# A Fourier-mixing block and its MLP: the first phase's loads, modulation rows, sequence matrices and negated halves in another order

## The chip, the cores and the metric

The kernel runs on one core of a Trainium2 chip. The metric is the time of one execution in microseconds (us) as the device counts it, median of several runs. Engines are called as the profile does: PE is TensorE (PEld its weight loads), DVE is VectorE, ACT is ScalarE, POOL is GpSimd, SP is SyncE, which only issues DMAs.

## The reference

Sequence length 2048, width 1024, MLP width 3584, all float32. The inputs are x, two pairs of DFT matrices (sequence and hidden), the MLP's weights and biases, a condition vector `c` and `w_mod`.

```
mod = (silu(c) @ w_mod).reshape(6, ...)
sa, ca, ga, sb, cb, gb = mod
h = layernorm(x) * (1 + ca) + sa
a = einsum("sd,ed->se", h, dft_hid_re);  b = einsum("sd,ed->se", h, dft_hid_im)
x = x + ga * (dft_seq_re @ a - dft_seq_im @ b)
h = layernorm(x) * (1 + cb) + sb
x = x + gb * (gelu(h @ w1 + b1) @ w2 + b2)
```

## The kernel before

All of it stands in one function, `fast()`. Work is written as small tasks, each with an engine, an assumed cost, the keys it waits for and a due time; a planner picks among the streams of tasks the one to emit next, and so fixes the order of each engine's queue at build time. Each engine works through its queue in that order. On-chip memory is one arena addressed by hand: `XR`, `EO`, `CRING`, `WRING`, `COP` and so on are offsets in it, and a task that writes a place waits for the last reader of what lay there before. SyncE issues nearly all loads; a load that must wait for its place holds up all loads behind it.

The first phase is what the change touches. It runs in these steps.

1. **Loads and mod.** Sixteen tiles of x (`load_x`, L2485, 128 x 1024 each), of which eight have a place at a time, and eight loads `wm` (L2496, 128 x 2048 each: the columns of `w_mod` for sa and ca). `mod_part` multiplies them by silu(c), part on TensorE, part on VectorE (L2534), which gives the shift and scale of the first LayerNorm as columns (L2584 to L2588).
2. **LayerNorm and folds.** The tiles are normalised, transposed by TensorE (L2685) and shifted and scaled. They are folded by their symmetry: `folds(cls)` adds and subtracts halves on VectorE (L2753, L2759, L2772) for two classes of sequence positions, ScalarE makes the fp16 high half of the result (L2778) and VectorE the low half (L2780). Key `("hop", cls, loc)` says that a part of the hidden operand is there.
3. **Modulation rows.** `row(n, j)` builds one row of mod (n = 0 to 3: ga, cb, sb, gb), spread over all partitions. Each row takes eight loads of 128 x 1024 (L2881, m = 0 to 31 in all) and eight pairs of float32 matmuls (L2887) that add up in one pair of PSUM banks. Key `("wru", m)` says that the place of load m has been read, `("rowe", n)` that row n was copied out. The loads go round in the places `WRING`. The gb row (n = 3) stands in the sequence stage and uses banks 0 and 1.
4. **Hidden DFT.** Eighteen units (`hid_unit`, L2956), each some 18 or 30 matmuls of fp16 in three passes (high times high, high times low, low times high); ScalarE and VectorE split each result again into fp16 halves (L2519, L2522). That is the right operand of the sequence DFT.
5. **Sequence matrices.** `cop_item` loads parts of the cosine and sine matrices in eight items (L2830) through the places `CRING`, two small ones (`dsp`, `csp`, L2795, L2811) before them, and splits them into fp16 halves at `COP`. The ring has six places, so that the last items wait until earlier ones were split (`("cru", n)`).
6. **Sequence DFT.** Sixteen tiles (`seq_tile`): 12 or 13 matmuls Q (L3038) and 24 to 26 matmuls P (L3026); ScalarE copies Q (L3043), VectorE forms P - Q and P + Q (L3048, L3053). The tiles 4 to 7 and 12 to 15 need part of the sequence matrix with the other sign. `neg_tasks` negates those parts in place on ScalarE (L2999), four instructions after tile 3 and four after tile 11, so tiles 4 and 12 wait for them.
7. **Second LayerNorm.** Pairs of finished tiles are multiplied by ga, added to x, normalised (L3097, L3115 to L3148), transposed (L3158), split (L3188, L3197, L3210). Each token's x + gb * b2 is stored too, where gb is needed (`gbb`).

Then the MLP: first layer (L3590) and second layer (L3699) as products of combined blocks in fp16 halves, with the splits of weights and activations on ScalarE (L2372) and VectorE (L2384, L2397), and the scales of the second layer (L3680). Both run on TensorE to the end of the kernel.

## Time and profile before

| what | value |
|---|---|
| median of 3 runs | 1428.72 us (1420.83 to 1430.15) |
| profiled execution, its own time | 1430.01 us |
| its span in the trace | 1428.2 us |
| mean granted clock of TensorE | 0.955 |
| busy: TensorE, VectorE, ScalarE, GpSimd | 1295.8, 1092.2, 749.7, 259.7 us |
| DMA moved | 302.30 MB, 212 GB/s over the span |
| first class-0 fold on VectorE (L2753) | at 72.87 us |
| first hidden matmul (L2956) | at 119.81 us |
| first sequence matmul (L3038) | at 188.94 us |
| first matmul of the MLP (L3590) | at 343.66 us |
| first second-layer scale delivered (L3680), eviction (L3739) | 428.59 us |

The page divides the span into 40 slices of 35.7 us and gives the busy share of each engine in tenths. A row of the timeline reads: start, duration, engine, line, operation, what it writes and reads, how many instructions were merged, and in brackets how long the engine stood idle before and what ended that. A row of windows gives, for a stretch of the span, its length, the busy time and number of instructions of each engine, TensorE's granted clock, the busy share of the DMA engines and the rate.

### The profile page before, as it was taken

What the parts mean: (1) busy time and instruction counts of PE and PEld (TensorE: products, weight loads), DVE (VectorE), ACT (ScalarE), POOL (GpSimd) and SP (SyncE); (2) the same over time, 40 slices, a digit from 0 to 9 for tenths busy, and PEclk for the clock granted to TensorE, in tenths of its full rate; (3) what the DMA queues carried; (4) which work ended last, traced back from release to release, by engine and by line L of the source; (5) the groups of instructions that cost most, each with busy time, mean ns of one, the idle gap of its engine ahead of it and who ended that gap; (6) DMA issues with size and microseconds to landing.
All of it is one profiled execution on the core that took longest, in us unless ns stands there. A gap on an engine that the chain in (4) does not pass through costs nothing.

```text
span 1428.2 us, 17336 instructions
## 1 busy us (share of the span) xinstructions
PE 1295.8 (91%) x6081; PEld 620.9 (43%) x6081; DVE 1092.2 (76%) x1623; ACT 749.7 (52%) x1188; POOL 259.7 (18%) x421
## 2 busy tenths in 40 slices
PE   5788588876969999999999999989999999999987
PEld 2545255543424444444444444434444444444433
DVE  5977677969697789889899897546585858675885
ACT  4685347776866746455555433346535353626330
POOL 2000010002101101010000000344534333543301
PEclk9899598998999999999999999999999999999999
DMA  9872334568456955676353546998877787876725
GB/s 369 322 251 83 88 134 91 157 216 310 142 204 192 255 164 183 204 186 216 137 181 125 192 172 240 305 314 282 287 261 249 241 279 261 281 254 209 235 81 112
DMA packets 108107, 302.30 MB, mean 212 GB/s; under 512 B 13900, under 2 KB 13900, under 8 KB 106088
## 3 DMA queue, kind: packets, MB, share of 16 engines
q1 hardware_dynamic: 75656, 195.63, 39.2%
q0 software_dynamic: 32352, 105.45, 24.9%
q8 instruction: 49, 0.80, 0.2%
q14 instruction: 50, 0.41, 0.1%
HBM read 216.10 MB, written 84.93 MB: 211 GB/s over the span
## 4 chain that ended last, share of the span: by engine, by line
PE 58%; DVE 4%; DMA 3%; issue 2%; ACT 1%; POOL 0%; SPq 0%; DVEq 0%; POOLq 0%; ACTq 0%
PE ps L3699 31%; PE ps L3590 26%; DVE arena L2384 1%; DMA arena<-in_cre_dram 1%; DVE arena L3749 1%; DMA arena<-in_w_dram 1%; DMA arena<-fw 1%; DVE arena L2397 1%; ACT arena L2372 1%; DMA fw<-arena 1%; DVE arena L3616 0%; POOL out_dram L3801 0%; POOL arena L3521 0%; ACT arena L3609 0%; ACT ps L3288 0%
## 5 line engine op out<-in xcount | busy, mean ns | idle before, releaser
L3590 PE MATMUL ps<-arena 128*128 128x512 f16 x2352 | 522.0, 384 | 28.8 <-ACT arena L3612 16.8
L3699 PE MATMUL ps<-arena 128*128 128x512 f16 x2352 | 515.4, 381 | 18.1 <-ACT arena L3739 14.2
L3590 PEld LDWEIGHTS <-arena 128*128 128x128 f16 x2352 | 232.7, 99 | 314.3 <-issue 42.9
L3699 PEld LDWEIGHTS <-arena 128*128 128x128 f16 x2352 | 231.1, 98 | 300.1 <-issue 25.1
L3749 DVE SCALAR_TENSOR_TENSOR arena<-ps,i4c,arena 128x1024 f32<-128x1024 f32 x179 | 229.4, 1282 | 101.6 <-PE ps L3699 98.5
L2372 ACT ACTIVATE arena<-arena,shc 128x512 f16<-128x512 f32 (+1 forms) x115 | 116.3, 1018 | 161.6 <-DVE arena L2397 94.2
L2384 DVE SCALAR_TENSOR_TENSOR arena<-arena,shc 128x512 f16<-128x512 f32 (+1 forms) x115 | 129.0, 1122 | 35.3 <-ACT arena L2372 34.9
L2397 DVE TENSOR_TENSOR arena<-arena 128x512 f32<-128x512 f32 (+1 forms) x196 | 149.1, 764 | 3.5
L3495 ACT ACTIVATE arena<-arena 128x512 f32<-128x512 f32 (+5 forms) x148 | 91.2, 617 | 104.9 <-DVE arena L3504 93.7
L3609 ACT ACTIVATE arena<-arena,b1s,i1c 128x512 f32<-128x512 f32 x78 | 63.4, 813 | 91.2 <-DVE arena L3616 91.2
L3504 DVE TENSOR_TENSOR arena<-arena 128x256 f32<-128x256 f32 x240 | 88.5, 420 | 14.8 <-DMA arena<-in_cre_dram 14.8
L3300 POOL PARTITION_ALL_REDUCE sums<-sums x21 | 11.0, 523 | 487.5 <-DVE sums L3296 487.5
L3616 DVE TENSOR_TENSOR arena<-arena,ps 128x512 f32<-128x512 f32 x78 | 53.4, 685 | 53.1 <-PE ps L3590 49.9
L2372 ACT ACTIVATE arena<-arena,s1c 128x512 f16<-128x512 f32 (+1 forms) x70 | 61.0, 885 | 59.8 <-DVE arena L2397 44.2
L2887 PE MATMUL ps<-arena,scol 128*128 128x512 f32 x128 | 63.6, 649 | 14.1 <-DMA arena<-in_wm_dram 11.2
L2384 DVE SCALAR_TENSOR_TENSOR arena<-arena,s1c 128x512 f16<-128x512 f32 (+1 forms) x70 | 66.5, 960 | 12.6 <-ACT arena L2372 12.4
L3521 POOL DMA_DIRECT2D arena<-in_cim_dram x99 | 53.7, 542 | 102.9 <-ACT arena L3495 97.1
L2384 DVE SCALAR_TENSOR_TENSOR arena<-arena,s2c 128x1024 f16<-128x1024 f32 x49 | 62.1, 1281 | 9.1 <-ACT arena L2372 9.0
L3521 POOL DMA_DIRECT2D arena<-in_cre_dram x99 | 54.2, 548 | 78.1 <-ACT arena L3495 58.8
L3288 ACT ACTIVATE ps<-arena 128x1024 f32<-128x1024 f32 x46 | 46.9, 1019 | 32.7 <-DMA arena<-in_w_dram 24.7
L3612 ACT ACTIVATE arena<-ps 128x512 f32<-128x512 f32 x78 | 45.9, 589 | 31.8 <-PE ps L3590 31.7
L2956 PE MATMUL ps<-arena 128*128 128x257 f16 (+5 forms) x297 | 45.8, 303 | 17.7 <-DVE arena L2522 10.5
(204 smaller groups left out, 1226.4 us busy)
## 6 DMA issues: line engine op xcount, KB each, us to landing
fw<-arena SPq DMA_DIRECT2D x73, 512.0 KB, 5.7
arena<-fw SPq DMA_DIRECT2D x112, 256.0 KB, 5.4
arena<-fw SPq DMA_DIRECT2D x49, 512.0 KB, 5.5
arena<-in_cre_dram POOLq DMA_DIRECT2D x96, 256.0 KB, 5.1
arena<-in_cim_dram POOLq DMA_DIRECT2D x96, 256.0 KB, 5.1
arena<-in_wm_dram SPq DMA_DIRECT2D x32, 512.0 KB, 5.8
arena<-in_w_dram SPq DMA_DIRECT2D x56, 256.0 KB, 4.4
arena<-in_w_dram SPq DMA_DIRECT2D x28, 512.0 KB, 6.3
```

The lines of the kernel that those rows point to most:

```text
L2372: act.activation(o[m][0], q(j), AF.Copy, **sc)
L2384: dve.scalar_tensor_tensor(o[m][1], q(j), scale, o[m][0], op0=ALU.mult, op1=ALU.subtract)
L2397: dve.tensor_tensor(q(d), q(a), q(b), op=op)
L2887: pe.matmul(bank((6 if n < 3 else 0) + h), scol[:, k : k + 1].to_broadcast([P, P]), FA(o + 512 * h, (1, 512)), start=k == 0, stop=k == 7,)
L3495: f = lambda: act.activation(sq(a), sq(a), AF.Square, accum_out=csum[0:pn, n : n + 1])
L3504: dve.tensor_tensor(a[:, o::2], a[:, o::2], b[:, o::2], op=op)
L3521: return lambda t: gp.dma_start(t[0:pn], v)
L3590: pe.matmul(ps.rearrange("p (k t) -> p k t", k=4), w1c[:, m, s, a, d * P : (d + 1) * P], zc(m)[:, b, :, d, :], start=(start and d == 0 and ...
L3609: act.activation(dst, src, AF.Gelu_apprx_tanh, scale=inv, bias=b1s[:, 2 * p + j : 2 * p + j + 1])
L3616: after_pe("dve", 0.6, lambda: dve.tensor_tensor(q, q, ps[b], op=ALU.add), kp[b])
L3699: pe.matmul(t[:, j], hidc[:, c_, m, a, k * P : (k + 1) * P], w2c[:, m, c_, w], start=(start and c_ == 0 and n == 0), stop=(c_ == 1 and n = ...
L3749: lambda: dve.scalar_tensor_tensor(dst, ps[b], inv, dst, op0=ALU.mult, op1=ALU.add), kp[b],
```

## The change

Line numbers shift: what stood at L2485 stays there, the wm loads move to L2499, row loads to L2885, row matmuls to L2891, sequence matrix loads to L2829, folds to L2752 to L2779, hidden matmuls to L2958, negations to L3004, sequence matmuls to L3032 and L3044, first and second layer to L3596 and L3705.

- x tiles 4 to 7 and 8 to 11 are loaded after the second and the fifth wm load, not behind all of them.
- `CRING` gets two more places (31984 and 33008, where x tiles lay); only the last two items, which take the places of the two small ones, wait for an earlier item to be split.
- Rows 2 and 3 load into other places: loads 16 to 19 into the second ring, 20 to 23 into freed places of normalised tiles and of x, 24 to 31 into the class-0 part of `EO` after the class-0 folds. The gb row's matmuls move to the hidden stage, into banks 6 and 7.
- The split of a class-0 fold waits for row load 11 and no longer for 19; that of class 1 waits for the last x tiles and two sequence items.
- The hidden units of a class come in another order: by `loc` first.
- The negated halves are written to places of their own (`NEG`), the first four before the first sequence tile, the other four after tile 7; tiles 4 to 7 and 12 to 15 read from there.
- Due times, the assumed cost of a row's matmuls (0.88 to 0.46), the place of gb's copy and of b2, and the waits of some later loads go with it.

```diff
-    CRING = (41996, 49172, 0, 1028, 2056, 3084)
+    CRING = (41996, 49172, 0, 1028, 2056, 3084, 31984, 33008)
-    WRING = [25792 + 1024 * n for n in range(4)], [34656 + 1024 * n for n in range(4)], (4160, 5184, 6208)
-    GBT = 19072
+    WRING = [25792 + 1024 * n for n in range(4)], [34656 + 1024 * n for n in range(4)]
+    GBT, B2T = 29920, 30944
-    COP = (102400, 69632)
+    COP, NEG = (102400, 69632), (8320, 102400)
...
     for k in range(8):
+        if k == 2 or k == 5:
+            for i in range(4 if k == 2 else 8, 8 if k == 2 else 12):
+                load_x(i)
         load(("wm", k), lambda k=k: sp.dma_start(wm2(k), wm[:, k, 0 : 2 * D]), cost=2.75)
-    for i in range(4, 8):
-        load_x(i)
...
-        o = CRING[n if n < 2 else (n - 2) % 6]
+        o = CRING[n if n < 2 else n % 8]
-        free = {0: [], 1: [], 2: [("cru", 0), *w1_made], 3: [("cru", 1)]}
-        deps = free.get(n, [("n", 11)] if n < 8 else [("cru", n - 6)])
+        free = {0: [], 1: [], 8: [("cru", 0), *w1_made], 9: [("cru", 1)]}
+        deps = free.get(n, [("n", 11)] if n < 6 else [("n", 15)])
...
-            h = add(f"foldh{cls}", "act", 2.0, ..., [ka, ("wru", 23 if cls else 19)], None, due)
+            h = add(f"foldh{cls}", "act", 2.0, ..., [ka, *(([("n", 15), ("wru", 23)] + [("cru", 6), ("cru", 7)] * loc) if cls else [("wru", 11)])], None, due)
...
-            split("cop", src, hi, lo, SC, [key, ("wru", 15), ("tpd", 3)], last, 1024, 58.0 + ch)
+            split(f"cop{ch // 2}", src, hi, lo, SC, [key, ("wru", 19), ("wru", 21), ("tpd", 3)], last, 1024, 38.0 if ch == 2 else 58.0 + ch)
...
-            elif 20 <= m < 24:
-                o, was = xr(m - 16), [("n", 15)]
+            elif m < 16:
+                o, was = WRING[m // 4 % 2][m % 4], [("wru", m - 8)] if m > 7 else w1_made
+            elif m < 20:
+                o, was = WRING[1][k], [("wru", m - 4)]
+            elif m < 22:
+                o, was = nr(m - 11), [("tpd", 2)]
             elif m < 24:
-                o, was = WRING[m // 4 % 2][m % 4], [("wru", m - 8)] if m > 7 else w1_made
+                o, was = xr(m - 18), [("n", 13)]
             else:
-                o, was = WRING[2][m % 3], [("wru", m - 3)] if m > 26 else hidend
+                o, was = eo(k // 4, k % 4, 0, 0), [("hop", 0, 0), ("hop", 0, 1)]
-                        bank((6 if n < 3 else 0) + h), scol[:, k : k + 1].to_broadcast([P, P]), FA(o + 512 * h, (1, 512)),
+                        bank(6 + h), scol[:, k : k + 1].to_broadcast([P, P]), FA(o + 512 * h, (1, 512)),
-            if k == 0 and n == 3:
-                deps.append(("y", 10))
-            add("rowp", "pe", 2 * FP, f, deps, ("wru", m), (45.0, 45.0, 39.0, 205.0)[n])
+            add("rowp", "pe", 2 * FR, f, deps, ("wru", m), (39.0, 39.0, 39.5, 63.0)[n])
...
-        for tp in range(2):
-            for t in range(2):
+        for loc in range(2):
+            for tp in range(2):
                 for c_ in range(2):
-                    hid_unit(tp, t, cls, c_)
+                    hid_unit(tp, tp ^ loc, cls, c_)
...
-                    "neg", "act", 1.0, lambda v=v: act.activation(v, v, AF.Copy, scale=-1.0),
-                    [("P", 8 * tp + 3), ("Q", 8 * tp + 3)], ("neg", tp, t, a), 75.0 + 11.0 * (8 * tp + 3),
+                    "neg", "act", 1.0, lambda v=v, w=w: act.activation(w, v, AF.Copy, scale=-1.0),
+                    [("P", 7), ("Q", 7)] if tp else hidend + copk, ("neg", tp, t, a), 76.0 + 11.0 * 8 * tp,
...
+        def left(t, a, ch):
+            return HA((neg if ti > 3 and ch > 1 else cop)(tp, t, a, ch, kk), (1, 128))
-        if ti == 3:
-            neg_tasks(tp)
+        if i == 0 or i == 7:
+            neg_tasks(i // 7)
...
-            load(("w1", g, m), f, ([("turn", 11)] if m < 4 else [("gbst", 0), ("gbst", 1)]) + [("w1s", g, q) for q in range(7)], cost=0.7, stream="wl", due=200.0)
+            load(("w1", g, m), f, ([("turn", 11)] if m < 4 else hidend) + [("w1s", g, q) for q in range(7)], cost=0.7, stream="wl", due=200.0)
```

How the instructions stand on three engines. Names in the rows are those of the program with a buffer number; `arena_65` is the arena, `scol_105` silu(c).

SyncE at the start of the program, before (L2489 loads raw w1, L2500 two parts of the hidden matrices):

```order
L2489 DMA arena_65<-in_w_dram 128x512 x4
L2496 DMA arena_65<-in_wm_dram 128x2048 x8
L2485 DMA arena_65<-in_x_dram 128x1024 x4
L2500 DMA arena_65<-in_dre_dram 128x2x513
L2500 DMA arena_65<-in_dim_dram 128x2x513
L2485 DMA arena_65<-in_x_dram 128x1024 x4
```

SyncE at the same place, after:

```order
L2489 DMA arena_65<-in_w_dram 128x512 x4
L2499 DMA arena_65<-in_wm_dram 128x2048 x2
L2485 DMA arena_65<-in_x_dram 128x1024 x4
L2499 DMA arena_65<-in_wm_dram 128x2048 x3
L2485 DMA arena_65<-in_x_dram 128x1024 x4
L2499 DMA arena_65<-in_wm_dram 128x2048 x3
L2501 DMA arena_65<-in_dre_dram 128x2x513
```

The last three wm loads now stand behind eight x tiles instead of none, and the hidden matrices behind all twelve tiles of x.

TensorE at the end of the LayerNorm transposes (L2685 before, L2684 after; L2719 and L2718 are the small ones of the one-row parts), where the hidden units begin. Before:

```order
L2887 MATMUL ps<-arena_65,scol_105 128x512 x16
L2685 MATMUL ps<-ident_97,arena_65 128x128 x24
L2887 MATMUL ps<-arena_65,scol_105 128x512 x8
L2685 MATMUL ps<-ident_97,arena_65 128x128 x24
L2887 MATMUL ps<-arena_65,scol_105 128x512 x2
L2685 MATMUL ps<-ident_97,arena_65 128x128 x8
L2887 MATMUL ps<-arena_65,scol_105 128x512 x2
L2956 LDWEIGHTS arena_65
L2956 MATMUL ps<-arena_65 128x257
```

After:

```order
L2684 MATMUL ps<-ident_97,arena_65 128x128 x8
L2891 MATMUL ps<-arena_65,scol_105 128x512 x8
L2684 MATMUL ps<-ident_97,arena_65 128x128 x24
L2891 MATMUL ps<-arena_65,scol_105 128x512 x8
L2684 MATMUL ps<-ident_97,arena_65 128x128 x32
L2718 MATMUL ps<-ident_97,arena_65 4x128 x8
L2958 LDWEIGHTS arena_65
L2958 MATMUL ps<-arena_65 128x257
```

Counted from the program's start, 44 row matmuls (22 loads of rows 0 to 2) stood ahead of the first hidden matmul, and now 32 do (16 loads); the last 32 transposes stand in one piece right ahead of it.

ScalarE around the split of the first class-0 fold (L2778 before, L2777 after; L2668 to L2672 and L2743 normalise and fold the special parts, L2698 shifts and scales a transposed tile, L2721 a one-row part). Before:

```order
L2668 ACTIVATE arena_65<-arena_65,lnc_18_138 128x2x256
L2669 ACTIVATE arena_65<-arena_65,lnc_18_138 128x2x256
L2672 ACTIVATE arena_65<-arena_65,lnc_18_138 128x4
L2743 ACTIVATE arena_65<-arena_65 64x2x257
L2778 ACTIVATE arena_65<-arena_65 128x8x257
L2698 ACTIVATE arena_65<-ps,mbias_111,mcol_108 128x512 x3
```

After:

```order
L2612 ACTIVATE lnc_18_138<-csum_136,eps_13_114 128x4
L2721 ACTIVATE arena_65<-ps,msp_109 4x512 x2
L2777 ACTIVATE arena_65<-arena_65 128x8x257
L2697 ACTIVATE arena_65<-ps,mbias_111,mcol_108 128x512 x3
L2667 ACTIVATE arena_65<-arena_65,lnc_18_138 128x2x256
L2668 ACTIVATE arena_65<-arena_65,lnc_18_138 128x2x256
L2671 ACTIVATE arena_65<-arena_65,lnc_18_138 128x4
L2667 ACTIVATE arena_65<-arena_65,lnc_18_138 128x2x256
```

The split stood behind the normalisation of the last tiles; now the latter (L2667 and on) come behind it.

TensorE in the middle of the hidden units, after: the block of the whole gb row.

```order
L2958 MATMUL ps<-arena_65 128x256
L2958 LDWEIGHTS arena_65
L2958 MATMUL ps<-arena_65 128x256
L2958 LDWEIGHTS arena_65
L2958 MATMUL ps<-arena_65 128x256
L2891 MATMUL ps<-arena_65,scol_105 128x512 x16
L2958 LDWEIGHTS arena_65
L2958 MATMUL ps<-arena_65 128x257
L2958 LDWEIGHTS arena_65
L2958 MATMUL ps<-arena_65 128x257
```

And TensorE in the sequence stage before, where the gb row stood between the transposes of the second LayerNorm (L3158) and the P and Q matmuls:

```order
L3158 MATMUL ps<-ident_97,arena_65 128x128 x8
L2887 MATMUL ps<-arena_65,scol_105 128x512 x6
L3158 MATMUL ps<-ident_97,arena_65 128x128 x8
L2887 MATMUL ps<-arena_65,scol_105 128x512 x6
L3158 MATMUL ps<-ident_97,arena_65 128x128 x8
L2887 MATMUL ps<-arena_65,scol_105 128x512 x4
L3038 LDWEIGHTS arena_65
```

Sixteen matmuls (eight pairs) in three pieces became one block behind the tenth of the eighteen hidden units.

82 lines of the change are left out of this document (42 added, 40 removed).

## The prediction

> **What bounds the kernel now.** I read the page first for the engines, then the windows by stage, the timeline of TensorE through the first phase, and the waits.
>
> ```profile
> PE 1295.8 (91%) x6081; PEld 620.9 (43%) x6081; DVE 1092.2 (76%) x1623; ACT 749.7 (52%) x1188; POOL 259.7 (18%) x421
> ...
> PE   5788588876969999999999999989999999999987
> ```
>
> The digits cover 35.7 us each. From the thirteenth on TensorE is full; what can be had lies in the first twelve, some 430 us. The windows cut them at the first fold, the first hidden matmul, the first sequence matmul, the first matmul of the MLP and its first second-layer eviction:
>
> ```profile
> core 0: us, PE busy (x) PEld busy (x) DVE busy (x) ACT busy (x) POOL busy (x), PEclk, DMA share, GB/s
> 0.00:72.87 72.87, 49.81 (x169) 27.04 (x170) 54.35 (x115) 42.06 (x76) 10.39 (x28) 0.91 0.91 347
> 72.87:119.80 46.93, 38.69 (x136) 20.48 (x135) 34.25 (x42) 33.92 (x53) 0.00 (x0) 0.93 0.75 240
> 119.80:188.90 69.10, 50.03 (x314) 28.32 (x313) 50.87 (x64) 29.14 (x38) 1.64 (x5) 0.78 0.22 63
> 188.90:343.60 154.70, 120.89 (x728) 77.90 (x728) 125.87 (x213) 103.25 (x158) 19.11 (x27) 0.90 0.57 172
> 343.60:428.40 84.80, 67.10 (x308) 31.23 (x308) 68.86 (x111) 65.46 (x88) 8.92 (x13) 0.92 0.57 200
> ```
>
> Five stages, none saturated: in each TensorE and VectorE wait for one another and for ScalarE. The hidden stage (119.8 to 188.9) idles 19.1 us on TensorE, the sequence stage 33.8, the start of the MLP 17.7. A gain before 430 us counts only if the later stages don't swallow it.
>
> **The change part by part.** *x between the wm loads.* Now TensorE's and VectorE's modulation product waits for the last wm tile, ahead of which stand no late x tiles:
>
> ```profile
> 5.92 7.62 SPq L2496 DMA_DIRECT2D arena<-in_wm_dram  x8
> 15.70 7.77 SPq L2485 DMA_DIRECT2D arena<-in_x_dram  x4
> ...
> 31.18 8.13 SPq L2485 DMA_DIRECT2D arena<-in_x_dram  x4
> ...
> 46.86 0.15 DVE L2588 TENSOR_TENSOR mbias<-mcol 128x2 f32<-128x2 f32 x1
> ...
> 72.87 4.62 DVE L2753 TENSOR_TENSOR arena<-arena 128x2048 f32<-128x2048 f32 x2
> ```
>
> Eight x tiles of 512 KB come ahead of the last three wm; at the window's 347 GB/s these 4.2 MB are 12.1 us, so mod is ready near 59 to 61 instead of 46.9. VectorE does the statistics of x meanwhile, which it did after, so its 54.35 us of work only change places in a window with 18.5 us idle. I take 3.5 us for the first fold (bounds 0 and 12.1).
>
> *Class-0 fold freed from modulation row 19.* The split of the folded half waits for TensorE's rows although it reads none of them; only its place does:
>
> ```profile
> 82.18 2.49 DVE L2772 TENSOR_TENSOR arena<-arena 128x1028 f32<-128x1028 f32 x2
> ...
> 104.80 1.91 ACT L2778 ACTIVATE arena<-arena 128x2056 f16<-128x2056 f32 x1
> ...
> 107.55 2.30 DVE L2780 TENSOR_TENSOR arena<-arena 128x2056 f16<-128x2056 f32 x1 [1.94 <-ACT arena L2698]
> ...
> 119.81 2.46 PE L2956 MATMUL ps<-arena 128*128 128x257 f16 x18
> ```
>
> The operand is made at 84.7 and split at 104.8. Now the split waits for row 11 only; with the 3.5 us above and what stands ahead of it on ScalarE it comes near 92, the low half near 96. The first hidden matmul does not gain all of these 13 us: in TensorE's order it stands behind the LayerNorm transposes of the class-0 tiles. I take 112.4, that is 7.4 earlier (bounds 0 and 13).
>
> *Rows 16 to 31 among the hidden units, no late sequence matrices.* Eight rows cost what this row says, 13.9 us, 1.74 each. Now only two rows lie in the hidden stage and the last eight, the gb row, in the sequence stage; afterwards sixteen lie here. In return the stage's largest wait goes: the last two sequence-matrix items, whose loads stand in SyncE's queue behind a wait for the fold.
>
> ```profile
> 78.86 13.90 PE L2887 MATMUL ps<-arena,scol 128*128 128x512 f32 x32
> ...
> 128.99 16.91 PE L2956 MATMUL ps<-arena 128*128 128x257 f16 x131
> ...
> 175.26 12.26 PE L2956 MATMUL ps<-arena 128*128 128x257 f16 x81 [10.53 <-DVE arena L2522]
> 188.94 1.24 PE L3038 MATMUL ps<-arena 128*128 128x512 f16 x5 [1.42 <-DVE arena L2522]
> ```
> ```profile
> 153.85 1.28 SPq L2489 DMA_DIRECT2D arena<-in_w_dram  x3
> ...
> 161.60 1.25 SPq L2830 DMA_DIRECT2D arena<-in_cre_dram  x2
> ```
>
> TensorE's work here becomes 50.0 − 3.9 + 16 × 1.74 = 74.0 us. New waits come in: all eight loads' matmuls of the gb row stand as one block behind the tenth unit; from the second on they wait for a class-1 fold on VectorE, the third class-1 combination waits for the seventh of them, and behind it stand the split, the low half and the units of the block's far side. I count 3.6 us idle before the rows and 5 behind, 8.6 together: 112.4 + 74.0 + 8.6 = 195.0 for the first sequence matmul, **6 us later** than now. Bounds: no idle, 186.4; idle as now (19.1), 205.5. I lean low, since the ring wait that made 10.5 us of it is gone. The eight loads of the gb row (4.2 MB, 12.1 us at 347 GB/s) move along in SyncE's queue; the windows' DMA share is 0.22 here, so their cover is this stage's idle DMA, and without it they would cost up to those 12.1. Behind them in the queue wait the raw w1 tiles and the next x reload, for which no matmul of this stage waits. The row's copy on ScalarE, 1.02 us, moves ahead of the first sequence tile, its stores to GpSimd's queue early in that stage, where 19.1 of 154.7 us are busy.
>
> On the price of a stop: in the rows below eight records after a 3.66 us wait take 6.10 us against 3.70 after 1.27. So each of the two stops may add up to 2.4 us. The Trainium skill ("TensorE: Matmul & The Clock Gate", Part 1) says that an idle window of about 3.4 us drops the clock to half until a further such window was busy; by it a long stop costs at most some 1.7 us more (estimate from that page), and the sum would be up to 3.4 us higher. The trace's 2.4 agrees in kind.
>
> *The sequence stage without the gb row and with the negated halves apart.*
>
> ```profile
> 210.93 2.95 ACT L2999 ACTIVATE arena<-arena 128x1024 f16<-128x1024 f16 x3 [1.74 <-PE ps L3026]
> ...
> 279.88 5.32 PE L2887 MATMUL ps<-arena,scol 128*128 128x512 f32 x12
> ...
> 286.93 1.88 PE L2887 MATMUL ps<-arena,scol 128*128 128x512 f32 x4
> ...
> 290.08 3.70 PE L2887 MATMUL ps<-arena,scol 128*128 128x512 f32 x8 [1.27 <-DMA arena<-in_wm_dram]
> ...
> 300.70 6.10 PE L2887 MATMUL ps<-arena,scol 128*128 128x512 f32 x8 [3.66 <-DMA arena<-in_wm_dram]
> ...
> 306.83 1.02 ACT L2910 ACTIVATE arena<-ps 128x1024 f32<-128x1024 f32 x1 [6.27 <-PE ps L2887]
> ...
> 343.66 1.87 PE L3590 MATMUL ps<-arena 128*128 128x512 f16 x4 [10.63 <-DVE arena L3053]
> ```
> ```profile
> 309.93 1.28 DVE L3135 SCALAR_TENSOR_TENSOR arena<-arena,lns 128x1024 f32<-128x1024 f32 x1 [7.45 <-ACT arena L3097]
> ```
>
> The gb matmuls take 5.32 + 1.88 + 3.70 + 6.10 = 17.0 us and wait 4.9 for DMA; ScalarE stands 6.3 behind their last record, and VectorE 7.4 behind ScalarE's next square. The eight negations are still made (1.04 each, four before the first tile instead of on the way to the fifth), so they only move; their 4 us cover is the first tiles' matmuls, and without it ScalarE's eviction of the first Q would be 4 us late. Upper bound: 17.0 + 4.9 + 4.2 = 26. But the stage is as much VectorE's: 125.9 of 154.7 us, and the change removes none of its work. In the changed order, six instructions of 1024 columns, four of 512 and four small ones that were done by the first MLP matmul come behind it, by the next fence's rows (1.22 and 0.69) and the 0.15 of the mod row 6 × 1.22 + 4 × 0.69 + 4 × 0.15 = 10.7 us. Were VectorE alone the bound, the stage would shrink by just these. I take the 17.0 of the matmuls, between 10.7 and 26: the stage ends at 195.0 + 137.7 = 332.7, **11 us earlier** than now.
>
> *What the MLP's start gives back.*
>
> ```profile
> 371.23 1.22 DVE L3197 TENSOR_TENSOR arena<-arena 128x1024 f16<-128x1024 f32 x1 [2.13 <-ACT arena L3188]
> ...
> 377.24 0.69 DVE L3885 TENSOR_TENSOR arena<-arena,ps 128x512 f32<-128x512 f32 x1 [3.39 <-PE ps L3590]
> ...
> 411.49 5.34 PE L3699 MATMUL ps<-arena 128*128 128x512 f16 x24
> ...
> 428.59 1.11 ACT L3739 ACTIVATE arena<-ps,i4c 128x1024 f32<-128x1024 f32 x1 [1.48 <-DVE i4c L3680]
> ...
> 429.76 2.72 PE L3699 MATMUL ps<-arena 128*128 128x512 f16 x6 [12.92 <-ACT arena L3739]
> ```
>
> TensorE has its first second-layer products at 417 and then waits 12.9 us for a scale that VectorE delivers at 428.4, at the end of its queue of splits. So this meeting place is VectorE's: its 68.9 us in 84.8 become 79.7, with 15.9 us idle to take the 10.7 up. Part of that idle is waiting for ScalarE's splits (the 2.13) and is filled, part for products that now come earlier too (the 3.39). I take half, **5 us given back** (bounds 0 and 10.7). From 430 on TensorE is full and its work the same; the gbb row's accumulating stores and the w1 loads move to places where DMA is busy 0.57 and less, so I give them nothing (2 us either way).
>
> Sum: +6 − 17 + 5 = −6 against the profiled execution's 1430.0 (span 1428.2): 1424. That execution lies 1.3 above the median of the three runs, 1428.7 (1420.8 to 1430.2), so for a median I name 1422.7; the rivals' times stand against 1428.7 too.
>
> **The rivals.**
>
> *A: VectorE fills its idle, and no stop in the hidden stage.* For it: the deferred work has 15.9 us of idle to fall into, and the ring wait is gone. Then the sequence stage starts at 190 (+1), shrinks by 17 and nothing but 1 us comes back: 1 − 17 + 1 = −15, 1413.7, and 1409.5 if the negations' 4.2 us are had as well. Against it: two instructions between the gb rows and the class-1 folds wait for each other.
>
> *B, the other side: the gb rows at the folds.* The block of eight rows stands in TensorE's queue and waits for VectorE's class-1 fold, and VectorE for the sixth row; all units behind come late. If the idle is the 19.1 us of now plus 2 × 2.4 slow restarts, the sequence stage starts at 210 (+21), saves only VectorE's 10.7 deferred us, and these come back by half: 21 − 10.7 + 5.4 = +16, 1444.7. With these savings it decides from an idle in the hidden stage of 8 us on, and is 1% from 22 us on. For it: stops in that stage were long before, clock 0.78. Against it: the fold's inputs are loaded earlier now.
>
> *C: it is hidden anyway.* VectorE is the bound from 189 to 428 (194.7 busy of 239.5). Its work is the same, the start 6 us later; what TensorE saves is idle elsewhere: +6 − 17 + 10.7 = 0, 1428.7. For it: the change takes nothing from VectorE. Against: its 44.7 us idle there, over half of it behind ScalarE.
>
> *D: mod is late.* The 12.1 us of x ahead of wm pass through whole: the first unit at 121 instead of 112.4, all else as forecast: −6 + 8.6 = +2.6, 1431.3. Against it: 18.5 us idle on VectorE in that window.
>
> **How the numbers follow.** Forecast 0.40 (its own range 1415 to 1430), A 0.27, C 0.15, D 0.06, B 0.12. Eight in ten from 1405 to 1439: left out are, below, the best part of A with terms near their bounds, and above, most of B. A difference of 1%, 14.3 us, is about what a measurement of this kernel tells from no change. Faster by more than that, below 1414.4: two thirds of A and a quarter of the forecast, 0.28; slower, above 1443: most of B and a little of C and D, 0.13; the rest 0.59.
>
> **What would show it.** Right: mod ready near 60; first hidden matmul near 112; no wait for the sequence matrices' split of 10 us; the first sequence matmul between 190 and 200; the next stage some 137 us, with no modulation rows in it; TensorE's wait for the first second-layer eviction longer than 12.9, ending near 423. Wrong: a first sequence matmul before 187 or after 203; a stage of more than 144 us (VectorE bound), or an MLP start whose 84.8 us do not grow; or a change after 430, where I expect none.

## The result: slower by 0.8%, and the profile after

The changed kernel takes 1438.5 us (median of 12 runs, 1434.7 to 1443.7), the kernel before 1427.5 (12 runs on the same chips, 1420.8 to 1432.9). The ratio is 1.0077, 95% interval 1.0057 to 1.0098: some 11 us slower, where 6 faster were forecast. The profiled executions have spans of 1438.2 and 1428.2 us.

From the page of the changed kernel the totals of the engines and TensorE's row of 40 slices:

```profile
PE 1303.0 (91%) x6081; PEld 625.5 (43%) x6081; DVE 1091.7 (76%) x1623; ACT 748.1 (52%) x1188; POOL 262.6 (18%) x421
...
PE   5798799877659899899999999979999999999987
```

The work is the same to 1%. The windows of the changed kernel are cut at the events of the prediction: first class-0 fold (rounded up), first hidden matmul, first sequence matmul, first MLP matmul, first second-layer matmul behind an eviction.

```profile
core 0: us, PE busy (x) PEld busy (x) DVE busy (x) ACT busy (x) POOL busy (x), PEclk, DMA share, GB/s
0.00:76.00 76.00, 47.83 (x155) 28.41 (x156) 54.43 (x115) 43.11 (x77) 10.39 (x28) 0.82 0.88 330
76.00:115.65 39.65, 33.55 (x135) 18.22 (x133) 29.25 (x36) 29.93 (x49) 0.00 (x0) 0.99 0.91 260
115.65:202.28 86.63, 76.04 (x362) 38.50 (x361) 53.85 (x64) 33.21 (x42) 2.20 (x6) 0.89 0.33 113
202.28:336.00 133.72, 107.48 (x697) 73.02 (x697) 120.42 (x210) 97.43 (x150) 15.72 (x21) 0.90 0.54 149
336.00:432.30 96.30, 67.69 (x309) 31.31 (x308) 76.58 (x126) 71.03 (x97) 12.08 (x17) 0.89 0.58 206
432.30:1438.00 1005.70, 970.39 (x4428) 436.06 (x4427) 757.18 (x1078) 473.39 (x777) 222.27 (x349) 0.98 0.66 216
```

The kernel before has these rows for the last two stretches (the prediction cut the first of them at 428.40, here it is cut at the matmul itself):

```profile
343.60:429.80 86.20, 67.14 (x309) 31.27 (x309) 69.02 (x112) 66.57 (x89) 8.92 (x13) 0.92 0.56 197
429.80:1428.00 998.20, 969.20 (x4428) 435.91 (x4427) 757.83 (x1081) 474.74 (x778) 219.65 (x349) 0.98 0.67 218
```

So the 10.0 us between the spans run up as follows (the change's event minus the same event before): first hidden matmul −4.2, first sequence matmul +13.3, first MLP matmul −7.7, first second-layer eviction +2.5, end +10.0. The first phase does bring 7.7 us; the 86.1 us behind it grow by 10.2, and the 998 us after that, whose matmuls are the same, by 7.5. TensorE's rows in the timeline of the changed kernel, the waits in brackets:

```profile
115.65 3.67 PE L2958 MATMUL ps<-arena 128*128 128x257 f16 x18
...
158.06 13.98 PE L2891 MATMUL ps<-arena,scol 128*128 128x512 f32 x28 [3.36 <-DVE arena L2771]
...
173.59 0.39 PE L2958 MATMUL ps<-arena 128*128 128x257 f16 x2 [1.55 <-ACT arena L2777]
...
177.18 22.62 PE L2958 MATMUL ps<-arena 128*128 128x257 f16 x130 [3.19 <-DVE arena L2779]
...
202.28 2.76 PE L3044 MATMUL ps<-arena 128*128 128x512 f16 x12 [2.49 <-DVE arena L2521]
...
432.31 19.98 PE L3705 MATMUL ps<-arena 128*128 128x512 f16 x84 [12.12 <-ACT arena L3745]
...
581.98 7.03 PE L3596 MATMUL ps<-arena 128*128 128x512 f16 x24 [4.58 <-ACT arena L3618]
...
659.81 7.03 PE L3596 MATMUL ps<-arena 128*128 128x512 f16 x24 [3.47 <-ACT arena L3618]
```

The gb rows stand in the hidden stage as forecast, with a stop of 3.36 us ahead of the last seven loads and 4.7 us in two pieces behind them. The last two rows are new: where the change waits 4.58 and 3.47 us at 582 and 660, TensorE ran through before:

```profile
542.69 36.42 PE L3590 MATMUL ps<-arena 128*128 128x512 f16 x168
...
619.16 36.42 PE L3590 MATMUL ps<-arena 128*128 128x512 f16 x168
```

ScalarE's rows show the stretch behind the first MLP matmul. First the change, then before. The two-instruction rows of ScalarE are the scaling of the last pair in the second LayerNorm (L3154, before L3148); the other one is the first split of 1024 columns of w1's third block.

```profile
371.35 2.37 ACT L3154 ACTIVATE arena<-arena,lns 128x1024 f32<-128x1024 f32 x2 [0.42 <-DVE lns L3152]
...
383.88 1.14 ACT L2372 ACTIVATE arena<-arena,s1c 128x1024 f16<-128x1024 f32 x1
```
```profile
367.89 2.36 ACT L3148 ACTIVATE arena<-arena,lns 128x1024 f32<-128x1024 f32 x2
...
383.71 1.14 ACT L2372 ACTIVATE arena<-arena,s1c 128x1024 f16<-128x1024 f32 x1
```

Counted from the first MLP matmul, the last pair is scaled 35.4 us in (371.35 − 336.00) against 24.2 (367.89 − 343.66): 11.1 us later. VectorE's busy time (the third of the pairs) up to that point grew by 9.7 us, first before, then the change:

```profile
343.66:367.89 24.23, 21.84 (x100) 10.16 (x99) 21.77 (x42) 21.24 (x33) 5.19 (x8) 0.94 0.83 285
```
```profile
336.00:371.35 35.35, 35.06 (x161) 16.34 (x159) 31.47 (x64) 25.79 (x43) 8.87 (x12) 0.94 0.85 299
```

Not all of that was deferred. Some 4 us of it are two passes of w1's split, two combinations of its blocks and two additions of the first MLP products, which stood behind the scaling before. By the windows VectorE's busy time ahead of the first MLP matmul fell by 7.4 us (265.3 to 258.0), where the prediction counted 10.7.

The split of w1 stands behind the scaling in ScalarE's queue and comes at 383.9 us (383.7 before), though the MLP begins 7.7 us earlier. From the scaling to that split it takes 12.5 us, 3.3 less than before, and from the split to TensorE's first matmul behind the eviction 48.4 us, 2.4 more. So the 10.2 us are 11.1 − 3.3 + 2.4.

### The profile page after: what moved, and what is told of

It reads as the page before. It is cut to its first block, busy times and chain, and to the rows that moved or that the text cites. A ratio compares the mean times of both kernels' runs of the same rounds, so it can differ in the third digit from the quotient of the medians.

```text
span 1438.2 us, 17292 instructions
## 1 busy us (share of the span) xinstructions
PE 1303.0 (91%) x6081; PEld 625.5 (43%) x6081; DVE 1091.7 (76%) x1623; ACT 748.1 (52%) x1188; POOL 262.6 (18%) x421
## 4 chain that ended last, share of the span: by engine, by line
PE 63%; DVE 8%; DMA 4%; ACT 3%; issue 2%; POOL 1%; SPq 0%; DVEq 0%; POOLq 0%; ACTq 0%
PE ps L3705 33%; PE ps L3596 28%; DMA arena<-in_w_dram 3%; DVE arena L2384 2%; DVE arena L2397 1%; DMA arena<-in_cre_dram 1%; PE ps L3032 1%; ACT arena L2372 1%; DVE arena L3755 1%; DVE arena L3203 1%; DVE arena L3216 1%; DVE arena L3145 1%; PE ps L3164 0%; ACT arena L3882 0%; ACT ps L3294 0%
## 5 line engine op out<-in xcount | busy, mean ns | idle before, releaser
L3596 PE MATMUL ps<-arena 128*128 128x512 f16 x2352 | 526.6, 386 | 35.8 <-ACT arena L3618 34.8
L3705 PE MATMUL ps<-arena 128*128 128x512 f16 x2352 | 512.6, 380 | 17.3 <-ACT arena L3745 13.8
L3596 PEld LDWEIGHTS <-arena 128*128 128x128 f16 x2352 | 233.6, 99 | 324.9 <-issue 56.5
L3705 PEld LDWEIGHTS <-arena 128*128 128x128 f16 x2352 | 230.4, 98 | 297.2 <-issue 20.5
L3306 POOL PARTITION_ALL_REDUCE sums<-sums x21 | 14.1, 672 | 498.6 <-DVE sums L3302 483.1
L3294 ACT ACTIVATE ps<-arena 128x1024 f32<-128x1024 f32 x46 | 46.9, 1018 | 39.5 <-DMA arena<-in_w_dram 30.9
L3618 ACT ACTIVATE arena<-ps 128x512 f32<-128x512 f32 x78 | 46.0, 590 | 36.5 <-PE ps L3596 36.5
L2891 PE MATMUL ps<-arena,scol 128*128 128x512 f32 x128 | 60.0, 615 | 3.4 <-DVE arena L2771 3.4
L3032 PE MATMUL ps<-arena 128*128 128x256 f16 (+3 forms) x400 | 51.7, 290 | 8.3 <-DVE arena L3059 8.3
```

Source lines behind the costliest of these rows:

```text
L2891: pe.matmul(bank(6 + h), scol[:, k : k + 1].to_broadcast([P, P]), FA(o + 512 * h, (1, 512)), start=k == 0, stop=k == 7,)
L3032: pe.matmul(PA(pb + o, (1, w)), l, r, start=n == 0, stop=n == len(mm_) - 1)
L3596: pe.matmul(ps.rearrange("p (k t) -> p k t", k=4), w1c[:, m, s, a, d * P : (d + 1) * P], zc(m)[:, b, :, d, :], start=(start and d == 0 and ...
L3705: pe.matmul(t[:, j], hidc[:, c_, m, a, k * P : (k + 1) * P], w2c[:, m, c_, w], start=(start and c_ == 0 and n == 0), stop=(c_ == 1 and n = ...
```

## The experiments

Three questions: what the hidden stage's 86.6 us are made of; why the stretch behind the first MLP matmul grows by 10.2 us; and what the 7.5 us after 432 are. All events by the first matmul of each stage in one profiled execution, in us; medians and ratios from the timed runs. A profiled span can lie some us from its kernel's median, so verdicts go by the ratio. An event can shift between executions of one order too: mlp_y has the change's order of instructions up to 330 us, and its sequence stage begins 3.5 us earlier.

| kernel | hidden | sequence | MLP | eviction | span | median | ratio to before (95%) |
|---|---|---|---|---|---|---|---|
| before | 119.8 | 188.9 | 343.7 | 429.8 | 1428.2 | 1427.5 | |
| after | 115.7 | 202.3 | 336.0 | 432.3 | 1438.2 | 1438.5 | 1.0077 (1.0057 to 1.0098) |
| fr88 | 109.1 | 190.8 | 342.6 | 436.8 | 1439.4 | 1438.6 | 1.0064 (1.0042 to 1.0085) |
| gb_hop1 | 114.3 | 190.0 | 341.6 | 435.6 | 1438.1 | 1439.7 | 1.0080 (1.0063 to 1.0096) |
| gb_seq | 112.5 | 189.0 | 366.7 | 462.2 | 1464.6 | 1465.8 | 1.0262 (1.0245 to 1.0279) |
| x_back | 119.5 | 196.3 | 331.7 | 428.0 | 1430.5 | 1437.3 | 1.0074 (1.0052 to 1.0096) |
| neg_inplace | 112.4 | 198.3 | 343.0 | 439.3 | 1434.0 | 1440.4 | 1.0105 (1.0073 to 1.0137) |
| b_hold | 118.1 | 194.0 | 343.4 | 439.1 | 1442.9 | 1440.3 | 1.0094 (1.0059 to 1.0129) |
| b_more | 119.5 | 188.6 | 342.8 | 440.2 | 1438.4 | 1439.7 | 1.0100 (1.0071 to 1.0129) |
| mlp_x | 115.7 | 202.3 | 336.5 | 433.3 | 1431.1 | 1432.8 | 1.0047 (1.0030 to 1.0065) |
| mlp_y | 113.1 | 198.8 | 336.7 | 430.4 | 1427.1 | 1428.7 | 1.0011 (0.9990 to 1.0032) |
| mlpx_x_back | 120.1 | 199.0 | 336.7 | 432.1 | 1429.5 | 1428.4 | 1.0016 (0.9997 to 1.0035) |
| mlpy_x_back | 119.7 | 198.0 | 334.4 | 428.8 | 1426.7 | 1423.8 | 0.9986 (0.9966 to 1.0006) |
| mlpy_gb_hop1 | 114.3 | 192.9 | 345.1 | 436.4 | 1429.5 | 1430.8 | 1.0024 (1.0003 to 1.0044) |
| mlpy_x_fr | 118.6 | 191.7 | 343.4 | 435.1 | 1429.0 | 1431.5 | 1.0027 (1.0003 to 1.0051) |

### The hidden stage: rows or stops?

**fr88**, on the change, gives the rows' matmuls the assumed cost of before, so that the planner puts them elsewhere; **gb_hop1** lets the gb row's loads wait for the class-1 splits, so that its matmuls come behind the hidden units; **gb_seq** takes the gb row back into the sequence stage, with three places of its own, and banks, due times and waits as before.

```diff
-    FP, FR = 0.88, 0.46
+    FP, FR = 0.88, 0.88                                  # fr88
...
-                o, was = eo(k // 4, k % 4, 0, 0), [("hop", 0, 0), ("hop", 0, 1)]
+                o, was = eo(k // 4, k % 4, 0, 0), [("hop", 1, 0), ("hop", 1, 1)]   # gb_hop1
+                o, was = (25792, 26816, 27840)[m % 3], [("wru", m - 3)] if m > 26 else hidend   # gb_seq
...
-                        bank(6 + h), scol[:, k : k + 1].to_broadcast([P, P]), FA(o + 512 * h, (1, 512)),
+                        bank((6 if n < 3 else 0) + h), scol[:, k : k + 1].to_broadcast([P, P]), FA(o + 512 * h, (1, 512)),   # gb_seq
```

> The change with one number back: the planner reckons a row's matmuls at 0.88 instead of 0.46 each (the trace has 1.74 to 1.98 us a load, two matmuls). The gb row's matmuls then stand in pieces, twelve of sixteen between the hidden and the first sequence tiles. Theory S (the block of gb rows between the class-1 folds makes VectorE and TensorE wait for each other): the two waits of 3.4 and 3.2 us in the hidden stage and VectorE's 11.1 us go, the first sequence matmul comes at about 193 instead of 202, and some 10 us of row matmuls go back into the sequence stage. Theory V (VectorE's and ScalarE's work, not TensorE's, sets the first second-layer eviction at 432): time within 3 us of the changed kernel's 1438. Rival P (the planner's wrong clock costs the time): faster by 5 to 10 us, 1428 to 1433, with the waits of 4.6 and 3.5 us after 540 us gone.

> The change with the gb row's loads held until the class-1 folds are split (no other edit). Its matmuls come behind the last hidden unit and among the first sequence tiles. Theory S: no mutual wait, the last hidden matmul ends near 185 instead of 200, the first sequence matmul near 190; the rows then delay the sequence stage by their own 14 us. Rival R (the rows' own 14 us is what makes the hidden stage long, not the waits): the first sequence matmul only some 7 us sooner, and the total as the changed kernel. In total theory V says within 3 us of 1438.

> The change with the gb row back in the sequence stage: due time, banks 0 and 1 and waits as in the kernel before, its loads in three places behind the hidden units. Theory S: the first sequence matmul near 185 (hidden stage shorter by 14 us of rows and the two stops); the first MLP matmul near 336 again, since the 17 us and the 5 us of DMA waits are back in the sequence stage. Theory V: total 1436 to 1441. If it comes to 1428 or less, the move of the gb row alone is the loss.

Without the block at the folds (gb_hop1) TensorE waits at the same place, and longer:

```profile
160.43 0.61 PE L2958 MATMUL ps<-arena 128*128 128x257 f16 x2 [9.75 <-ACT arena L2777]
...
164.01 22.52 PE L2958 MATMUL ps<-arena 128*128 128x257 f16 x130 [2.97 <-DVE arena L2779]
```

The sequence stage begins 12.3 us earlier than in the change, about the 14.0 us of the 28 row matmuls. So the stop was not the row block's price: the class-1 folds would have been waited for anyhow, and the block filled part of that wait. The slow clock behind the stop (shown below) comes without the block too. What the block costs is its own time. gb_seq says the same (−13.3), and fr88 −11.5. None of it reaches the end: gb_hop1's and fr88's sequence stages take 151.6 and 151.8 us against 133.7, and the totals cannot be told from the change's. In both, six of the gb row's eight loads are now multiplied behind the first sequence tile; gb_hop1:

```profile
195.48 10.46 PE L2891 MATMUL ps<-arena,scol 128*128 128x512 f32 x24
```

So some 10 of the 18 us are the rows themselves, moved into the next stage; what the other 8 are was not isolated. gb_seq I had wrong: its sequence stage takes 177.7 us, with waits of the transposes for ScalarE's splits of up to 11 us, of which the last is this:

```profile
364.89 1.97 PE L3166 MATMUL ps<-ident,arena 128*128 128x128 f32 x8 [11.27 <-ACT arena L3170]
```

It carries several edits and a new order, so it says nothing on what the gb row alone would cost there.

### The order of x, and the negated halves

**x_back** loads x tiles 4 to 7 behind all wm loads and 8 to 11 behind the two loads of the hidden matrices, as before. **neg_inplace** writes the negated halves over the originals again, behind the tiles that read them.

```diff
-        if k == 2 or k == 5:
-            for i in range(4 if k == 2 else 8, 8 if k == 2 else 12):
-                load_x(i)                                # x_back: both groups behind the loop
...
-                v, w = HA(cop(tp, t, a, 2), (1, 1024)), HA(neg(tp, t, a, 2), (1, 1024))
+                v = w = HA(cop(tp, t, a, 2), (1, 1024))  # neg_inplace
...
-        if i == 0 or i == 7:
-            neg_tasks(i // 7)
+        if ti == 3:
+            neg_tasks(tp)
```

> The change with all late x tiles loaded behind the wm loads as before. The forecast had put the x order at a loss of 3.5 us in the first fold and rival D at 8.6. Theory S and V: mod ready 12 us sooner, first hidden matmul within 4 us of 115.7 either way (rows and transposes stand ahead of it), total within 4 us of 1438. Rival D: first hidden matmul near 107, total near 1430.

> The change with the negated halves in place as before, four after tile 3 and four after tile 11; all else as changed. If keeping them apart bought the forecast's 4 us, the first MLP matmul comes at 340 instead of 336, through a wait of TensorE ahead of tiles 4 and 12. Rival (the negations lie beside other work anyway): 336 plus or minus 1. The total follows the order at the MLP's start, so 1437 to 1442.

In x_back mod is ready at 48.7 us (in the change at 61.1, as forecast), and yet its first hidden matmul is at 119.5, later than the 115.7 of the change: a mod 12 us earlier did not bring that unit forward. x_back moves the late x tiles too, so it does not show what mod alone would do; in the change 54.6 us lie between mod and that unit. Its total is the change's. In neg_inplace the sequence stage takes 144.7 us against 133.7, with waits for the scaling of a pair that the change has not or has shorter (its row near 231.8 waits 1.97):

```profile
229.70 1.97 PE L3164 MATMUL ps<-ident,arena 128*128 128x128 f32 x8 [5.05 <-ACT arena L3154]
...
275.57 1.97 PE L3164 MATMUL ps<-ident,arena 128*128 128x128 f32 x8 [4.89 <-ACT arena L3154]
```

So with the separate places goes a stage shorter by 11 us, by this row of the table; its MLP starts at 343.0, where I had expected 340. The order of the tasks around it differs too, so I cannot say how much of the 11 is the dependency and how much the order. The total again does not move by what the interval can show.

### The stretch behind the first MLP matmul: is the deferred work paid in full?

**b_more** is the kernel before with nine further passes of VectorE over the ga row in place (a maximum of the tile with itself, which leaves it unchanged), three behind each of the three additions of the first MLP products: about 11 us.

```diff
-            f = lambda: dve.tensor_tensor(q, q, ps[b], op=ALU.add)
+            def f():
+                dve.tensor_tensor(q, q, ps[b], op=ALU.add)
+                for _ in range(3 if g == 0 else 0):
+                    dve.tensor_tensor(ga_t, ga_t, ga_t, op=ALU.max)
```

> The kernel before with nine more VectorE instructions of 1024 columns (1.22 us each, 11 us; a maximum of the ga row with itself, which changes no value) behind the first block's three additions, where the change has its deferred 10.7 us. All else in order as before. Rival W (amount: VectorE's extra work between the first MLP matmul and the first second-layer eviction passes through): eviction at 437 to 441 instead of 430, total 1435 to 1439. Theory O (order alone: VectorE's 15.9 us of idle there take the work up): eviction at 430 to 434, total within 4 us of the kernel before.

```profile
351.45 3.74 DVE L3888 TENSOR_TENSOR arena<-arena 128x1024 f32<-128x1024 f32 x3
...
377.59 2.37 ACT L3148 ACTIVATE arena<-arena,lns 128x1024 f32<-128x1024 f32 x2 [6.68 <-DVE lns L3146]
...
394.15 1.14 ACT L2372 ACTIVATE arena<-arena,s1c 128x1024 f16<-128x1024 f32 x1
...
440.19 5.24 PE L3699 MATMUL ps<-arena 128*128 128x512 f16 x12 [12.92 <-ACT arena L3739]
```

Eleven us of VectorE's work make the last pair's scaling 9.7 us later (377.59 against 367.89), the split of w1 10.4, the first second-layer eviction 10.4 and the whole 14 by the ratio (10 to 18 by its interval; 10.2 between the profiled spans). Counted from the first MLP matmul, which comes 0.8 us earlier here, the stretch grows from 86.1 to 97.4 us. None of VectorE's 17 us of idle took anything up. It is idle that lies behind ScalarE and TensorE in a chain that goes through VectorE itself: the rows show ScalarE standing 6.68 us for the LayerNorm's small VectorE instruction, and everything after it shifted.

### After 432: the order of the MLP

The planner decides the first phase and the MLP's first tasks together until a switch, from which the second layer's order follows rules. In its own clock the first block's first product is now done at 318.8 us (before 340.0), and at the switch 8, 23 and 24 tasks of w1, w2 and hid are left over (before 3, 17 and 21). The earlier MLP in that clock cannot by itself be the reason for what is left: for fr88 and gb_seq the planner has that product at 337.9 and 361.4 and leaves 8, 23 and 24 too, for neg_inplace at 323.1 and leaves 8, 19 and 24. **mlp_x** and **mlp_y** put out, on the change, fourteen of these tasks ahead of the switch, in the order of before: mlp_x right at the switch, mlp_y ahead of the last group of gelus. **b_hold** is the converse: the kernel before with its first phase as it was, but these tasks held back until the switch.

```diff
+    emitted(("zt", NS - 2))                              # mlp_y; mlp_x without this line, just ahead of the switch
+    for name in ('w2', 'w2', 'w2', 'w2', 'w2', 'w1', 'hid', 'w1', 'w2', 'w1', 'w1', 'w1', 'hid', 'hid'):
+        n = len(streams[name])
+        while len(streams[name]) == n:
+            force(streams[name], streams[name][0])
```
```diff
+    HELD = {'n1_2': 8, 'w1_2': 8, 'n2_0': 23, 'w2_0': 23, 'hid0': 24, 'hid1': 24}    # b_hold
...
+            if t.tag in HELD and len(q) <= HELD[t.tag]:
+                continue
```

> The change, with fourteen tasks of the MLP's start (splits and scales of the third block of w1, of the first block of w2 and of the first activations) emitted ahead of the planner's switch to its second rule, in the order in which the kernel before had them there; from some 90 instructions of VectorE on, the order of VectorE and ScalarE is then that of the kernel before. First phase untouched. Theory P (the loss lies in the order that the planner makes at the MLP's start: from the first MLP matmul to the end the four kernels with the change take 1096 to 1102 us, the kernel before 1084.5): the waits of 11.8, 4.6 and 3.5 us go, the time from the first MLP matmul falls by 10 to 17, total 1421 to 1428. Theory V (VectorE's amount of work sets the eviction at 432): unchanged, 1436 to 1440.

> The kernel before, with the same tasks of the MLP's start held back until the planner's switch, so that as many are left there as in the change (8, 23 and 24 instead of 3, 17 and 21); its first phase is that of before. Theory P: the first MLP matmul stays near 344, the rest takes 1096 to 1102 instead of 1084.5, total 1438 to 1445. Theory V: within 3 us of 1428.

> The change, with the same fourteen tasks of the MLP's start emitted before ScalarE's last four gelus of the first two blocks instead of behind them; the planner's switch then finds as much left as in the kernel before (3, 17, 21). Theory O (order: the splits stand behind the gelus, so that their chain starts at 384 although the MLP starts 7 us earlier): ScalarE's first split of the third block of w1 comes at 376 to 379 instead of 384, the first second-layer eviction at 425 to 428 instead of 432, total 1424 to 1428, as or faster than the kernel before. Rival W (the 10.7 us of VectorE's work that the change moved behind the first MLP matmul keep VectorE busy until 378 anyway): the eviction stays at 431 to 434, total 1431 to 1434 as with the tasks behind the gelus.

Windows of mlp_x, the last two stretches:

```profile
336.50:433.30 96.80, 68.54 (x309) 31.62 (x308) 74.39 (x120) 70.14 (x95) 12.60 (x17) 0.87 0.56 201
433.30:1431.00 997.70, 969.52 (x4428) 435.86 (x4427) 758.07 (x1081) 474.60 (x778) 219.43 (x349) 0.98 0.67 218
```

and of b_hold:

```profile
343.40:439.10 95.70, 68.27 (x308) 31.45 (x308) 70.84 (x113) 67.57 (x91) 8.46 (x13) 0.87 0.52 180
439.10:1442.00 1002.90, 968.79 (x4428) 435.66 (x4427) 757.00 (x1078) 473.29 (x777) 222.33 (x349) 0.98 0.66 217
```

mlp_x has the last stretch of before again (997.7 against 998.2) with the changed first phase; b_hold has 5.3 of the change's 7.5 us of growth there (1003.8 to the end of its span, which its window cuts 0.9 us early) with its MLP beginning where that of before does (343.4), and the same new waits in its timeline:

```profile
390.09 1.14 ACT L2375 ACTIVATE arena<-arena,s1c 128x1024 f16<-128x1024 f32 x1
...
586.93 6.84 PE L3593 MATMUL ps<-arena 128*128 128x512 f16 x24 [4.12 <-ACT arena L3615]
...
664.59 7.03 PE L3593 MATMUL ps<-arena 128*128 128x512 f16 x24 [3.48 <-ACT arena L3615]
```

What TensorE waits for there can be read on ScalarE, in the change and then before:

```profile
579.05 1.03 ACT L3294 ACTIVATE ps<-arena 128x1024 f32<-128x1024 f32 x1 [6.20 <-DMA arena<-in_w_dram]
...
581.35 0.58 ACT L3618 ACTIVATE arena<-ps 128x512 f32<-128x512 f32 x1
```
```profile
571.89 0.58 ACT L3612 ACTIVATE arena<-ps 128x512 f32<-128x512 f32 x1
...
584.21 1.03 ACT L3288 ACTIVATE ps<-arena 128x1024 f32<-128x1024 f32 x1 [3.94 <-DMA arena<-in_w_dram]
```

In the change the last copy of first-layer products out of PSUM (L3618) ahead of that wait, on which the matmul at 581.98 waits, stands behind a sum of squares over a raw weight tile (L3294), and that stood 6.20 us for the tile's load; before, the same copy (L3612) was done ahead of such a wait. At 660 the change shows the same with 4.36 us, b_hold ahead of 586.93 with 5.10. Across the fifteen kernels both waits of TensorE stand in the change, fr88, gb_hop1, gb_seq, x_back and b_hold, whose end lies 1002 to 1006 us after the eviction, and in none of the other nine (993 to 998 us; neg_inplace, with four fewer of the w2 tasks left over, is one of them).

So most of the 7.5 us belongs to the order of tasks across the switch and not to loads or stores that the change moved. b_hold shows a second price of that order: the split of w1 slips behind the gelus (390.09 for 383.71) and the stretch before 439 grows to 95.7 us with VectorE's work hardly changed (70.84 for 69.02). mlp_y, with that split ahead of the gelus, still makes it at the old time:

```profile
383.97 1.14 ACT L2372 ACTIVATE arena<-arena,s1c 128x1024 f16<-128x1024 f32 x1
```

since it stands behind the last pair's LayerNorm as well (I had expected 376 to 379). Its stretch is 93.8 us, its end 996.7 us after the eviction. From the split to the matmul behind the eviction it takes 46.5 us, as before (46.1) and not as in the change (48.4). So of the 10.2 us by which the change's stretch grew, 7.7 stay with the old order of these tasks and 2.5 go with it. Since b_hold grows by 9.6 without any deferred work, the two causes do not simply add. In all mlp_y takes 1428.7 us, 9.8 less than the change and not to be told from before. mlp_x, for which I had 1421 to 1428, takes 1432.8: its stretch stays at 96.8 us, with the wait of 11.8 us in it (12.2), and its interval still meets the change's.

### Together

mlp_y with x loaded as before, with the gb block behind the folds, or with both x and the old cost of rows; and mlp_x with x as before (edits as above).

> The change with the late x tiles behind the wm loads and with the fourteen tasks emitted ahead of the switch. Alone the x order gave a first MLP matmul at 331.7. Theory P: that start plus 1085 to 1090, 1417 to 1424, faster than the kernel before. Theory V: 1434 to 1438.

> The same with the late x tiles loaded behind the wm loads. With the tasks behind the gelus it took 1428.4. Theory O: 4 to 6 us less, 1422 to 1425, faster than the kernel before. Rival W: 1427 to 1430.

> The same fourteen tasks before the last gelus, x as in the change, the gb row's loads held until the class-1 folds. Alone the latter gave 1439.7 with a first MLP matmul at 341.5, 5.5 later than the change. Theory O: the split chain follows the MLP's start, so 5 us later than the variant without the hold, 1429 to 1433. Rival W: the chain has its own time, within 2 us of the variant without the hold.

> The change with the late x tiles behind the wm loads, the fourteen tasks ahead of the last gelus, and the planner's cost of a row's matmuls back at 0.88. With the last alone the first sequence matmul came at 190.8 instead of 202.3, but the first MLP matmul at 342.6 instead of 336. If an earlier first phase pays once the order is mended: 1419 to 1422, faster than the kernel before. Rival W (ScalarE's and VectorE's work between the first MLP matmul and the first second-layer eviction sets the latter, whatever the first phase): 1423 to 1427, within 3 us of the same kernel without the cost.

mlpy_x_back has the lowest median, 1423.8 us, beside 1427.0 for the kernel before; its interval, 0.9966 to 1.0006, includes 1. It is 1% below the change, and no run shows a version that beats the kernel before. Two forecasts missed here: mlpx_x_back takes 1428.4 us (1417 to 1424 expected), and mlpy_x_fr 1431.5 us, outside both of its theories: an earlier first sequence matmul (191.7) brought no earlier MLP (343.4). With x as before, mlp_x and mlp_y each lie 4 to 5 us lower, with intervals that meet or overlap: a hint that x between the wm loads costs something, not shown.

## Why the prediction was wrong

**The clock of the first phase held in its sum.** I said: the sequence stage "ends at 195.0 + 137.7 = 332.7, 11 us earlier than now". It ended at 336.0, 7.7 earlier.

- *First hidden matmul 112.4*: 115.7. The cause I named for lateness, mod, came when I said (61.1) and was not shown to cost anything: without the new order of x mod came at 48.7 and the unit at 119.5 (x_back). Rival D, which needs 121 here, falls.
- *74.0 of TensorE's work and 8.6 idle in the hidden stage*: 76.0 and 10.6. The wait of 10.53 us for the sequence matrices is gone as forecast, and the stops were where I put them, before and behind the gb rows. Of the 76.0, 7.7 us are slow clock (see the next point), as was part of the 50.0 that I started from (granted clock 0.78 in that stage), so the near match is partly chance. That they were a price of the rows was wrong: without the rows the wait is longer (gb_hop1). With the 3.3 us of the first unit, the sequence stage began at 202.3, 7 us late on the forecast.
- *A stop's slow restart, up to 2.4 us each*: too small. The windows of the change over the seven row loads behind the first stop, and over the units behind the second, the latter cut where the granted clock (third column from the end) returns:

```profile
158.06:172.04 13.98, 13.98 (x28) 5.83 (x28) 2.43 (x2) 0.42 (x1) 0.00 (x0) 0.88 0.00 0
177.18:189.18 12.00, 12.00 (x51) 5.81 (x52) 7.03 (x6) 1.50 (x3) 0.00 (x0) 0.50 0.49 175
189.18:199.80 10.62, 10.61 (x80) 6.73 (x79) 8.31 (x17) 6.88 (x12) 0.95 (x2) 0.96 0.16 52
```

  The kernel before ran such units at the full clock:

```profile
128.99:145.90 16.91, 16.84 (x132) 10.34 (x130) 14.95 (x15) 7.93 (x10) 0.00 (x0) 1.00 0.00 1
```

  The rows take 13.98 us where 28 at the 13.90 / 32 of before would take 12.2: 1.8 more. The units take 22.6 us for 130, against 16.7 at the 16.91 / 132 of before: 5.9 more, at a clock of 0.50 for 12.0 us though TensorE was busy throughout. gb_hop1 has the same behind its stop:

```profile
164.01:176.01 12.00, 12.00 (x51) 5.84 (x52) 7.03 (x6) 1.50 (x3) 0.00 (x0) 0.50 0.75 283
```

  The Trainium skill ("TensorE: Matmul & The Clock Gate", Part 1) has the clock return after some 3.4 us of work. The first stop agrees with that; behind the second it took 12.0 us, and the measurement decides. The order of instructions alone does not fix it. The kernel before ran 81 matmuls behind its wait of 10.53 us in 12.26 us (the row at 175.26 in the prediction), with the granted clock at 0.50 for the first 3.5 us; b_hold, whose order is the same up to the MLP, ran them with it at 0.50 for the first 12.0 us:

```profile
175.22 17.37 PE L2959 MATMUL ps<-arena 128*128 128x257 f16 x81 [11.06 <-DVE arena L2525]
```

- *Sequence stage −17.0*: −21.0 (133.7 for 154.7), between my 17 and the bound of 26. I counted the negated halves as 4.2 us at most; neg_inplace lengthens the stage by 11.0, order of tasks included. That VectorE's work moves behind the first MLP matmul held, with a smaller amount than the 10.7 us that I counted: its busy time ahead of that matmul fell by 7.4, and grew by 7.6 in the stretch behind it.

**The step that failed first is "I take half, 5 us given back (bounds 0 and 10.7)".** It was 10.2, near the upper bound. I had reckoned that 15.9 us of idle must take up something. The idle was the wrong thing to look at: the last pair's LayerNorm stands at the end of the deferred work, ScalarE's split of w1 behind that, and the second layer's first eviction behind the split. Work put ahead of such a chain comes out at its end nearly whole, whatever idle VectorE has further on (b_more: 11.0 in, the eviction 10.4 later). In the change the deferred work was 7.4 us, and 7.7 us of the stretch's growth stay when the tasks behind it have their old order (mlp_y); the other 2.5 go with that order, which is the next step. That 10.2 lies so near to my 10.7 is chance: the work was less than I counted, and the order added to it. (Two figures of the prediction are off by a tenth, 79.7 for 79.6 and 44.7 for 44.8, which changes nothing.) The event by which I meant to see it, TensorE's wait before that eviction, did not grow (12.12 us for 12.92), as TensorE was late too.

**The step that failed altogether is "From 430 on TensorE is full and its work the same ... I give them nothing (2 us either way)".** It was +7.5. I argued from work and DMA, and both were as I said. The planner had emitted fewer of the MLP's tasks before its switch, so the order of VectorE and ScalarE afterwards is another: ScalarE's copies for TensorE stand behind weight tiles that have not landed, with waits of 4.58 and 3.47 us that were not there. mlp_x and mlp_y take that away on the change (997.7 and 996.7 us after the eviction; 6 and 10 us in all by the medians), b_hold puts 5.3 us of it into the kernel before. Why the planner emitted fewer stays open; that its own clock has the MLP 21 us earlier is not enough, as fr88 and gb_seq show. The new order could be read before any run, and I looked at the first phase only.

In sum, against the profiled 1430.0 or the median: +13.3 − 21.0 + 10.2 + 7.5 = +10.0, where I had +6 − 17 + 5 + 0 = −6. Of the two rivals on the slower side, D had its reason in mod, and B had the sign and not the mechanism: the idle of the hidden stage stayed at 10.6 us, not 19 and more. C, hidden anyway, was the nearest: with the switch mended (mlp_y) the deferred work eats the gain and the total is that of before, 1.0011.

What stays open: which of the tasks across the switch puts the copies at 582 and 660 behind the weight tiles (they were moved fourteen at a time); whether the order of x costs the 4 to 5 us; and the gb row alone in the sequence stage, which gb_seq did not isolate.

## What to carry to other kernels

Work that is deferred behind a stage boundary is not paid from the idle time of its engine but from the chain that it is put in front of: follow what stands behind it in that engine's queue to the next meeting place, and count it in full unless that chain has slack. Where a planner or a table sets the order, compare the order on every engine to the end of the program, and above all across the place where its rules switch: a change of the first phase can reorder tasks hundreds of us away from the edit. And before a block of work is blamed for the wait beside it, ask what would be waited for without it.
